# First batch's token softmax built from scores with tokens in partitions, in two halves; seven low-word additions moved from VectorE to GpSimd; the order written anew

## The chip, the cores and the metric

One core of one Trainium2 chip runs the kernel. The metric is the device time of one execution in microseconds; the time of a kernel is the median over several runs. Engines are named as the profile names them: PE (TensorE, its matmuls), PEld (TensorE, its weight loads), DVE (VectorE), ACT (ScalarE), POOL (GpSimd), SP (SyncE, which here issues most loads and stores).

## What is computed

A cross attention between tokens `x` (8 batches, 8 heads, 512 tokens, 64 wide) and states (8 batches, 8 heads, 32 states, 64 wide), and then a feed-forward block over the joined rows:

```
scores  = x @ state^T / 8         a  = softmax over the 32 states      xread = a  @ state
scores2 = state @ x^T / 8         a2 = softmax over the 512 tokens     sread = a2 @ x
rows = concat(xread, sread) by batch, heads joined: 8 x 544 rows of 512
h = rows @ w_in (512 x 2048);  g = h * erf(softplus(h));  out = g @ w_out (2048 x 512)
```

`softplus(h)` is the reference's `max(h,0) + log1p(exp(-|h|))`. Inputs of the attention are float32. The two weight matrices arrive as 64-bit floats and are turned into float32 in the kernel.

## The kernel before

The output rows are worked off batch by batch. The first half of the columns of `w_in` (with the first half of the rows of `w_out`) is pass A, the second half is pass B; stores of B are added to those of A in DRAM. `xread @ w_in` is never formed in two matmuls: for each batch the state is multiplied into `w_in` first (steps `A1m`, `B0m` and so on, buffer `m`), and that is multiplied with the softmaxed scores `y`. Large products go through a Strassen-like scheme of seven products in place of eight (lines 690, 743, 813).

**Batch 0 in pass A is different**, since at the start nothing is loaded: it is done directly, as soon as pieces of weights arrive. This opening, about the first 60 us, is what the change touches. Its steps, by the names that the order uses:

- `lx0`..`lx3` load x of batch 0 (tokens in partitions, two heads each); `lst0` its states; `i0l0`..`i3l1` load the raw 64-bit words of four pieces of `w_in`, `o0l0`..`o3l1` those of `w_out`.
- A piece is converted by `convert` (line 370) in four operations: `a0` (ACT, line 374) from the high words, `a1` (ACT, 376) scales the low words, `v0` (DVE, 378) shifts by three bits, `v1` (DVE, 380) adds the low word. Piece `i0` is done in two halves, `i0` and `i0+`; the others, 128x1024 each, at once.
- `x0`..`x3` (PE, 445) transpose x of two heads each, four 128x128 transposes, into PSUM; `x0c`..`x3c` copy to SBUF (three by DVE, one by ACT). `s0`, `s0c` do it for the states.
- `q0`, `q1` (PE, 460) are the scores of four heads each with states in partitions: 16 matmuls with a 64x32 stationary tile and 128 tokens moving. `q00c` and so on copy them to SBUF.
- `tm0`, `tm1` (PE, 465) transpose these scores, so that tokens stand in partitions. Then comes the softmax over states, once for each group of four heads: `max` (481), `less` (482), `exp` (ACT, 483), `sum` (485), `inv`, `norm` (487); `ta0`, `ta1` (PE, 465) transpose the result back, and `ta0c`, `ta1c` (ACT) copy it to `y`.
- `big0`, `big1`, `big`, `wt`, `wz`, `wn`, `tw` (lines 493 to 506) make the other softmax, over tokens; `rd0` (PE, 525) reads with it.
- `n00`, `n01`, `n02` (piece `i0`, `i0+`, `i1`) and `n10`, `n12` (`i2`, `i3`) multiply the states into `w_in` (PE, 948).
- `h0`..`h7` (PE, 959) are eight products of 128 columns of h for all 512 tokens: two matmuls of 128x128 by 512 each, one for either group of heads. `h0s` is its softplus (ACT, 679), `h0c` its copy (ACT), `h0e` erf for two of them and `h0g` the product with h (DVE, 240).
- `o00`, `o02`, ... (PE, 980) multiply with `w_out`. `a1...` is the attention of batch 1, `A1m` its `m`, `A1f..` its h. `ub` (PE, 1047) turns the states of batch 1. `t..` steps and `T1`..`T4` form sums of `w_out` pieces on DVE.
- `~7*4` is four matmuls of the identity into bank 7: filling that keeps PE running while nothing else is ready. Its line is 427, like that of `warm`.

**What sets the order.** `ORDER` (line 20) is a list of all steps, written out; line 1129 issues them in that order, and `in_order` (line 1120) ties each instruction to the one before it on its engine. So every engine works strictly in the order of the list, and a step that waits holds up all later steps of its engine. Data dependencies across engines become semaphore waits. Loads are issued by SP in the order of the list, too.

Of the kernel before, what the change touches and what calls it, by code (L numbers as in the profile page):

```python
# [10 lines left out]
ALU = mybir.AluOpType  # L11
# [7 lines left out]

ORDER = """  # L20
warm lx0 lst0 lx1 lx2 lx3 i0l0 i0l1 i1l0 i1l1 x0 s0 x1 s0c x0c i2l1 x2 x1c q0 x2c i2l0 x3 q01c
q00c i0a0 big0 tm0 ls1 x3c i0v0 i0a1 max0 q1 i0v1 q11c i3l1 q10c less0 i0+a0 ~7*4 n00 tm1 big1
exp0 i0+v0 i3l0 i0+a1 sum0 big i1a0 inv0 max1 a1xq5 norm0 i1a1 less1 ~6*12 ta0 i1v0 exp1 a1xq4
n00c1 n00c0 sum1 ta0c wt0 inv1 norm1 i2a1 ~7*9 ub i1v1 ta1 i2a0 a1xq1 i0+v1 n02 ta1c i2v0 a1xq0
n02c0 ~6*2 n01 wt1 i2v1 h0 a1xq6 n01c0 i3a0 n01c1 o1l1 wz n02c1 n10 o0l1 i3a1 i3v0 o0l0 h1 n10c1
a1xq7 n10c0 i3v1 h0c o1l0 a1xq3 y01 ~7*2 n12 wn0 h0s h5 y02 h1c n12c1 a1tx2 n12c0 h1s wn1 tw0
a1tx0 tw1 ubc a1xq2 h0e h3 o2l0 tw0c h0g o2l1 tw1c o3l1 o0a0 rd0 a1tx3 y04 o0a1 o0v0 h4 a1x1 rn0
yl0 o1a0 o0v1 rt0 o1a1 h2 o1v0 a1tx1 rc0 o1v1 a1s h5s t01 h7 T1 h5c a2xq2 a1c1 a1c0 o3l0 t02 h3c
t31 a2xq6 h6 hold a1tu0 h3s lst7 h2c a1mx0 lst4 h7c a1tu1 o20 lst1 h4s t32 a2xq1 h7s lst5 a1sb0
h6s a1mx1 a2xq5 lst8 h2s o00 a1my1 lst2 t04 y03 lst3 h2e t34 A1m yk0 a1sb1 lst6 a1x3 h2g t3k a1x2  # L30
a1ex1 a1my0 o02 a1ex0 a1sm1 h4c a1sm0 h6c o10 A1m11 a1iz a1nm1 A1m00 A1m10 a2xq3 a1nm0 a1ey0 o22
a1ta1 a1ey1 a1ta0 a1x0 A1M1 o2a0 A1f01 y11 a1ty1 A1m01 A1f05 a1ty0 A1f0c o2a1 o12 A1M2 a1kz y12
a2xq0 y13 A1M4 t0k A1f06 o2v0 h4e u0 A1M3 y14 A1f02 A1f0u2 a1iy h4g o3a0 A1f07 A1f0c11 o2v1 u1
A1f0u3 A1f11 a1z1 o3a1 A1f0c22 a1z0 A1f04 a1z3 o3v0 h6e a1z2 a2tx0 A1f03 yk1 a2xq4 A1f0c21 o24
o3v1 A1f1c a2xq7 A1f0c12 A1f16 t1k u0c A1f0s22 T2 A1f12 A1f1u2 A1f0s21 A1f17 h6g A1f1c11 A1f0s11
rd1 A1f0s12 u1c t11 A1f1u3 A1f15 T4 a2x3 rn11 rn10 rt1 A1f14 t12 t2k t61 A1e0 o04 a2x2 A1f1c22 t41
a2tx2 A1f13 rc1 A1f1c21 A1g0 a2s o06 A1f1s12 a3xq1 a2c0 A1f1c12 a2c1 a3xq5 t14 A1f1s22 o26 t21
# [12 lines left out]
y33 t54 A3f06 a3ty1 A1bp21 A3M3 A3f0u2 a3kz A3f02 A1bu3 A3M4 a4xq2 A1bc11 A3f07 A1b4 A3f0c11  # L50
A1bc22 A1bp40 A3f0u3 y34 A1b4+ A2e0 A1bp41 A3f0c22 A3f11 A2g1 A3f04 A1bp30 A3f0c21 a3z2 a3iy A3f1c
A3f03 A2g0 a3z0 a3z3 A3f16 A1d3 a3z1 A1bp31 A1d0 A3f1u2 A3f12 A3f0c12 A2q A3f17 A3f1c11 A1bc21
A2ap10 A1bc12 A3f1u3 A2A1 A3f15 A1d1 yk3 A2ap50 a4tx2 A3f0s11 A3f0s12 A3f14 A1D0 A1U2 A2ap11
A3f1c22 A2A3 rd3 A2ac a4tx0 A2ap20 rn31 A1D1 rn30 rt3 A2a2 A2ap21 yl3 rc3 A3f0s21 a4x1 a4s A3f1s11
a4x0 A2A2 A3f1c21 A2ap60 a4c0 A1U3 a4c1 A2ap61 A2a3 A1D2 A3f1s22 A3f1s12 A3f13 a4tu0 A2ap51 A2au2
A1D4 A3f1c12 A2ac11 A2ap70 a5xq2 a4mx0 A3f1s21 A2ap71 A2A4 a5xq7 A1D3 A2bp10 A2au3 A3f0s22 a4sb0
A4m a5xq1 A2a4 a4ex0 A2bp11 A2ac22 A2ap40 A4m00 a5xq6 a4sm0 A4m11 A2ap41 A4m01 A2b2 A4m10 A2ap30
A2ac21 a4iz A2ap31 a4my0 A2bc a5xq5 A2bp20 a4nm0 A2bp60 A3e0 A2ac12 A2bp21 a4ta0 A2bp61 A2bp50
a5xq4 A4M1 A2bc11 A4f01 A2bu2 y41 a4x2 A4M3 A2bp51 a5xq0 A4f0c A4f05 y42 A2b4+ A4M2 A4f02 A2b3
a4ey1 a4x3 A4f06 A2d3 y43 a4ey0 A2bp70 a4ty1 A2d0 A4f0u2 a4ty0 A2bp71 A2b4 A4f07 a4kz A2bu3 y44  # L60
a5xq3 A4f0c11 A2bp40 A4M4 A4f0u3 a4iy A2bc22 A2bp41 A4f0c22 A4f11 A3g0 A3e1 A4f04 A4f03 A2D0
# [12 lines left out]
A5f14 rn51 rn50 A5f1s11 rt5 A5f0s12 A5f1c22 A4ap50 A3D1 rc5 a6tx2 A5f1s22 A4ap11 a6x1 A5f0s22 a6x3
A4a2 A5f13 A4ac a6s A4A2 A4ap60 a6c1 A5f1c12 A5f0s21 A4ap61 A4a3 a6c0 A5f1c21 A4ap20 a7xq0 a6tu0
# [107 lines left out]
def kernel(  # L183
# [8 lines left out]
    nc = tc.nc  # L192
# [971 lines left out]
```

## Time and profile before

| what | value |
|---|---|
| median of 3 runs | 686.01 us (685.63 to 686.43) |
| the profiled execution, its own time | 685.9 us |
| its span, first to last instruction | 684.1 us |
| PE busy over the span | 676.2 us (99%) |
| DVE, ACT, POOL busy | 591.4, 490.9, 87.8 us |
| granted PE clock | 1.00 throughout |
| mean DMA rate | 127 GB/s |

The profile is of one execution. A row of groups gives line, engine, operation, what is written and read, shapes, count, then busy time and mean duration of one, then the engine's idle time ahead of it. The windows view gives the busy time of each engine in a stretch. An instruction's duration contains about 0.09 us in which the next one on the same engine has already started, when nothing makes that one wait; so a queue of DVE instructions moves on by the duration less 0.09. A float32 matmul appears as two records, a transpose as one.

### The profile page before, as it was taken

What the parts mean: (1) busy time and instruction counts of PE and PEld (TensorE: products, weight loads), DVE (VectorE), ACT (ScalarE), POOL (GpSimd) and SP (SyncE); (2) the same over time, 40 slices, a digit from 0 to 9 for tenths busy, and PEclk for the clock granted to TensorE, in tenths of its full rate; (3) what the DMA queues carried; (4) which work ended last, traced back from release to release, by engine and by line L of the source; (5) the groups of instructions that cost most, each with busy time, mean ns of one, the idle gap of its engine ahead of it and who ended that gap; (6) DMA issues with size and microseconds to landing.
All of it is one profiled execution on the core that took longest, in us unless ns stands there. A gap on an engine that the chain in (4) does not pass through costs nothing.

```text
span 684.1 us, 13797 instructions
## 1 busy us (share of the span) xinstructions
PE 676.2 (99%) x5568; PEld 586.8 (86%) x5568; DVE 591.4 (86%) x772; ACT 490.9 (72%) x764; POOL 87.8 (13%) x84
## 2 busy tenths in 40 slices
PE   9999999999999999999999999999999999999997
PEld 7536478989888898999998889898989898989996
DVE  6899999999999999998896699697858795979793
ACT  5999948779787768856785975777674948676821
POOL 0020000030201202021200013010202020201103
PEclk9999999999999999999999999999999999999999
DMA  9896745697777777685975246131514323231427
GB/s 300 203 266 171 153 141 112 182 181 153 182 137 190 118 176 148 185 205 142 214 226 161 78 119 103 34 60 43 60 57 56 72 30 77 29 57 16 78 55 124
DMA packets 145839, 87.15 MB, mean 127 GB/s; under 512 B 92784, under 2 KB 138096, under 8 KB 145776
## 3 DMA queue, kind: packets, MB, share of 16 engines
q1 hardware_dynamic: 126720, 67.78, 36.0%
q0 software_dynamic: 18512, 17.96, 20.4%
q8 instruction: 44, 0.72, 0.4%
q10 hardware_dynamic: 544, 0.52, 0.2%
q14 instruction: 19, 0.16, 0.1%
HBM read 46.14 MB, written 40.11 MB: 126 GB/s over the span
## 4 chain that ended last, share of the span: by engine, by line
PE 88%; ACT 6%; DVE 3%; DMA 1%; issue 1%; SPq 0%; DVEq 0%; ACTq 0%
PE b L813 47%; PE b L690 25%; PE b L743 5%; PE b L1020 4%; PE b L641 4%; DMA big<-in_moe_w_out_dram 1%; ACT ring L679 1%; ACT ring L246 1%; PE b L525 1%; PE b L550 1%; PE b L427 1%; ACT ta L374 0%; ACT L679 0%; ACT ring L974 0%; ACT L575 0%
## 5 line engine op out<-in xcount | busy, mean ns | idle before, releaser
L246 ACT COPY ring<-b 128x512 f32<-128x512 f32 (+1 forms) x144 | 82.4, 584 | 97.5 <-PE b L690 69.5
L813 PE MATMUL b<-big,ring 128*128 128x128 f32 x1196 | 151.9, 275 | 0.0
L721 POOL DMA_DIRECT2D out_dram<-res x67 | 80.3, 1380 | 546.0 <-DVE res L238 150.1
L813 PEld LDWEIGHTS b<-big,ring 128*128 128x128 f32 x1196 | 145.7, 192 | 5.3 <-issue 2.5
L690 PE MATMUL b<-y,m 128*128 128x256 f32 x480 | 121.8, 381 | 0.4 <-DVE y L246 0.3
L690 PEld LDWEIGHTS b<-y,m 128*128 128x128 f32 x480 | 86.2, 190 | 12.4 <-issue 1.6
L246 ACT COPY res<-b 128x512 f32<-128x512 f32 (+2 forms) x125 | 64.2, 524 | 44.7 <-PE b L813 30.7
L690 PE MATMUL b<-sy,m 128*128 128x256 f32 x360 | 91.7, 380 | 0.0
L240 DVE TENSOR_TENSOR ring<-ring 128x2048 f32<-128x2048 f32 (+1 forms) x36 | 78.0, 2167 | 5.2 <-ACT ring L698 3.0
L679 ACT ACTIVATE ring<-ring 128x512 f32<-128x512 f32 x128 | 76.5, 631 | 2.5 <-DVE ring L238 2.1
L813 PE MATMUL b<-ta,ring 128*128 128x128 f32 x548 | 72.8, 276 | 0.0
L690 PEld LDWEIGHTS b<-sy,m 128*128 128x128 f32 x360 | 65.2, 190 | 8.7 <-issue 1.4
L813 PEld LDWEIGHTS b<-ta,ring 128*128 128x128 f32 x548 | 68.0, 192 | 5.4 <-issue 1.7
L238 DVE TENSOR_TENSOR ring<-ring,b 128x512 f32<-128x512 f32 (+1 forms) x72 | 47.2, 660 | 27.7 <-ACT ring L246 10.2
L813 PE MATMUL b<-big,ta 128*128 128x128 f32 x572 | 70.8, 275 | 0.0
L813 PEld LDWEIGHTS b<-big,ta 128*128 128x128 f32 x572 | 68.1, 192 | 2.4 <-ACT b L246 0.8
L239 DVE TENSOR_TENSOR ring<-ring 128x1024 f32<-128x1024 f32 (+3 forms) x66 | 68.6, 1050 | 0.1
L238 DVE TENSOR_TENSOR res<-res,b 128x512 f32<-128x512 f32 (+2 forms) x60 | 36.2, 604 | 29.4 <-ACT res L246 14.2
L698 ACT ACTIVATE ring<-ring 128x2048 f32<-128x2048 f32 x30 | 57.4, 1914 | 0.2
L246 ACT COPY b<-b 128x512 f32<-128x512 f32 (+2 forms) x63 | 34.4, 546 | 14.1 <-PE b L690 8.0
L238 DVE TENSOR_TENSOR res<-res 128x512 f32<-128x512 f32 (+1 forms) x56 | 41.8, 751 | 1.6 <-ACT res L246 1.0
L238 DVE TENSOR_TENSOR ring<-ring 128x1024 f32<-128x1024 f32 (+1 forms) x35 | 39.8, 1141 | 1.0 <-ACT ring L246 0.6
(145 smaller groups left out, 967.7 us busy)
## 6 DMA issues: line engine op xcount, KB each, us to landing
out_dram<-res POOLq DMA_DIRECT2D x63, 256.0 KB, 5.3
out_dram<-res SPq DMA_DIRECT2D x32, 256.0 KB, 3.0
big<-in_x_dram SPq DMA_DIRECT2D x30, 256.0 KB, 4.2
big<-in_x_dram SPq DMA_DIRECT2D x112, 64.0 KB, 3.4
big<-in_moe_w_in_dram SPq DMA_DIRECT2D x12, 512.0 KB, 6.3
big<-in_moe_w_out_dram SPq DMA_DIRECT2D x12, 512.0 KB, 4.9
kept_y<-y SPq DMA_DIRECT2D x8, 512.0 KB, 4.0
y<-kept_y SPq DMA_DIRECT2D x8, 512.0 KB, 4.1
```

Of the source, the lines that this page charges most:

```text
L238: add = lambda o, a, b: tt(o, a, b, op=ALU.add)
L239: sub = lambda o, a, b: tt(o, a, b, op=ALU.subtract)
L240: mul = lambda o, a, b: tt(o, a, b, op=ALU.mult)
L246: do[name] = lambda: f(*args)
L641: pe.matmul(out=to[j][k][Ns * p:Ns * p + Ns, :], lhsT=by, rhs=w_in[r, 4 * j:4 * j + 4, i, :], start=True, stop=True)
L679: act.activation(out=o, in_=i, func=ACTF.Softplus)
L690: pe.matmul(out=to[:, i], lhsT=xs[n - 1][:, q:q + P], rhs=ys[n - 1], start=(start and i == 0), stop=(i == 1), skip_group_check=True)
L698: step(u + "e%d" % o, lambda s=s: act.activation(out=s, in_=s, func=ACTF.Erf))
L721: nc.gpsimd.dma_start(out=to, in_=of, accum_op=ALU.add)
L743: pe.matmul(out=to[:, E2 * h:E2 * h + E2], lhsT=a[:, k // 2, k % 2], rhs=rhs[n][:, k], start=(start and h == 0 and k == 0), stop=(k == 3), ...
L813: pe.matmul(out=out_[:, P * j:P * j + P], lhsT=lhs[:, i], rhs=rhs[:, i], start=(start and j == 0 and i == 0), stop=(i == 1), skip_group_ch ...
L1020: pe.matmul(out=to[:, P * i:P * i + P], lhsT=xs[n - 1][:, i, k], rhs=ys[n - 1][:, k], start=(start and i == 0 and k == 0), stop=(k == 1), ...
```

## The change

**Token softmax.** `tm0` and `tm1` go. New steps `t0`, `t1` compute the scores a second time, with tokens in partitions: `t0` for one half of the tokens (`k` = 0), `t1` for the other, each 16 matmuls with 64x128 of the turned x stationary and 32 states moving, alternating between the upper and the lower 64 rows of PE. The softmax is now done by halves of tokens and not by groups of heads; `max` and `less` are split in two (128x256 each), the rest is as wide as before. `ta0` gives `y` for tokens of the first half, for all heads, so that each `h` product can be split in a left and a right half of the tokens (`h0L`, `h0R`).

**Transposes of x by halves.** `x00`, `x01` and so on: two transposes each and a 128x256 copy each, four by DVE and four by ACT.

**Low words by GpSimd.** In seven pieces (`i1`, `i2`, `i3`, `o0`..`o3`) the step `v1` is issued on POOL.

**Others.** The softmax over tokens works in place; some PSUM banks are named anew; the whole `ORDER` list is another one.

```diff
+BY_GPSIMD = ("i1", "i2", "i3", "o0", "o1", "o2", "o3")
...
-    def convert(name, to, words):
+    def convert(name, to, words, adder=None):
...
-        step(name + "v1", lambda: tt(d, d, lo, op=ALU.add))
+        step(name + "v1", lambda: (adder or dve).tensor_tensor(d, d, lo, op=ALU.add))
...
+        def token_score(k):
+            for h in range(H):
+                at = P * where[h][0] + Ns * where[h][1]
+                for j in range(2):
+                    r = slice(D * j, D * j + D)
+                    pe.matmul(out=token[k, j][:, at:at + Ns], lhsT=xT0[r, h, k],
+                              rhs=st00[r, Ns * h:Ns * h + Ns], start=True, stop=True)
...
+        for k in range(2):
+            step("t%d" % k, token_score, k)
         for g in range(2):
             step("q%d" % g, score, g)
+        for k in range(2):
+            M, Z = (t[:, k].rearrange("p (j f) -> p j f", j=2) for t in (M1, Z1))
+            for j in range(2):
+                of = token[k, j].rearrange("p (f n) -> p f n", n=Ns)
+                step("max%d%d" % (k, j), lambda M=M, of=of, j=j: dve.reduce_max(
+                    out=M[:, j], in_=of, axis=AX.X))
+                step("less%d%d" % (k, j), lambda M=M, of=of, j=j, k=k: sub(
+                    A0[:, k, j].rearrange("p g (q n) -> p (g q) n", n=Ns), of,
+                    M[:, j].unsqueeze(2).to_broadcast([P, H, Ns])))
...
-            step("tm%d" % g, four, bank[6 + g], lambda c, g=g: sc0[:, g, c])
...
-        def first(g, i, to):
+        def first(g, i, to, part):
+            at = slice(256 * part, 256 * part + 256)
             for e in range(2):
-                pe.matmul(out=to, lhsT=X[2 * g + e][:, P * i:P * i + P], rhs=y[0][:, e],
-                          start=(e == 0), stop=(e == 1))
+                pe.matmul(out=to[:, at], lhsT=X[2 * g + e][:, P * i:P * i + P], rhs=y[0][:, e, at],
+                          start=(part == 0 and e == 0), stop=(e == 1), skip_group_check=True)
```

The order of the opening on PE was `x0 s0 x1 x2 q0 x3 tm0 q1 ~7*4 n00 tm1 ~6*12 ta0 ~7*9 ub ta1 n02 ~6*2 n01 h0 n10 h1 ~7*2 n12 h5 tw0 tw1 h3 rd0 h4 rt0 h2 a1s h7 h6 o20 o00 A1m o02`. It becomes `x00 s0 x10 x01 x30 x11 x20 x31 x21 t0 t1 q0 q1 ~7*3 n01 ~7*7 n00 ~7*2 ta0 ~7*7 ta1 h0L n02 ub h0R h1L h1R n10 h2L h3L h3R n12 h2R tw1 tw0 h4L h5L rd0 h7L rt0 h5R a1s h6L h4R h7R h6R o00 ~7*3 o10 A1m`. On DVE, from the first `max` on: `max00 max01 less00 less01 max10 max11 less10 less11 sum0 i0v0 inv0 i0v1 norm0 sum1 q00c inv1 i1v0 norm1 n00c1 q01c big1 big0 big n01c1 i2v0 y01`. On ACT, from the first conversion on: `i0+a0 i0+a1 x21c i0a0 exp0 i0a1 exp1 q10c n01c0 i1a0 i1a1 q11c n00c0 ta0c i2a0 i2a1 ta1c wt1 wt0 i3a0 n02c0 i3a1 h0c`. On POOL: `i1v1 i2v1 i3v1 o0v1 hold lst8 o1v1`, then the other loads `lst`, `o2v1`, `o3v1`.

More of the change, by code (lines that the diff above doesn't have):

```diff
@@ L17 @@
 TWICE = 1
+BY_GPSIMD = ("i1", "i2", "i3", "o0", "o1", "o2", "o3")
 ORDER = """
[L21 to L37, printed above, removed]
@@ L968, in first_unit @@
                 to = bank[k % 6]
-                step("h%d" % k, first, g, i, to)
+                for part in range(2):
+                    step("h%d%s" % (k, "LR"[part]), first, g, i, to, part)
                 step("h%ds" % k, soft, s[:, k], to)
```

357 lines of the change are left out of this document (187 added, 170 removed).

## Prediction

> **What bounds the kernel now.** I read the windows view first. Its columns are: stretch and length in us, then the busy time of PE, PEld, DVE, ACT and POOL with the number of instructions, the granted clock, the DMA share and GB/s.
>
> ```profile
> 0.00:10.00 10.00, 8.55 (x86) 7.07 (x94) 3.72 (x8) 3.03 (x4) 0.69 (x6) 1.00 0.85 268
> 10.00:20.00 10.00, 9.43 (x132) 8.04 (x128) 9.86 (x21) 8.77 (x16) 0.00 (x0) 1.00 1.03 296
> 20.00:30.00 10.00, 10.00 (x94) 4.98 (x79) 8.26 (x18) 9.82 (x16) 0.00 (x0) 1.00 0.77 212
> 40.00:50.00 10.00, 9.42 (x51) 3.58 (x50) 9.20 (x18) 9.94 (x17) 4.51 (x8) 1.00 1.16 268
> 60.00:100.00 40.00, 39.65 (x245) 24.43 (x245) 39.25 (x57) 31.49 (x49) 0.00 (x0) 1.00 0.58 145
> 100.00:200.00 100.00, 100.00 (x990) 87.97 (x989) 98.04 (x124) 77.37 (x129) 12.16 (x10) 1.00 0.74 161
> ```
>
> From 100 us on PE never stops, so the rest of the program lasts as long as its matmuls do. What an edit of the opening is worth is how much earlier PE has its work done when that stretch begins. In the opening a busy PE says little, because filling counts as busy. So I read the timeline of PE next (start, length, line, operation, tiles, shapes).
>
> ```profile
> 13.79 1.50 PE L427 MATMUL b<-ident 128*128 128x128 f32 x12
> 15.28 0.66 PE L465 MATMUL b<-ident,ring 128*128 128x128 f32 x4
> 15.88 2.27 PE L427 MATMUL b<-ident 128*128 128x128 f32 x18
> 18.08 0.45 PE L1047 MATMUL b<-ident,st 128*64 128x64 f32 x8
> 18.49 0.66 PE L465 MATMUL b<-ident,ring 128*128 128x128 f32 x4
> 19.72 0.67 PE L948 MATMUL b<-w_in,st 64*32 64x256 f32 x16 [0.57 <-DVE w_in L380]
> 20.96 0.45 PE L948 MATMUL b<-w_in,st 64*32 64x128 f32 x16
> 21.34 1.98 PE L959 MATMUL b<-y,m 128*128 128x512 f32 x4
> ```
>
> Line 427 is filling, 465 at 15.28 and 18.49 is `ta0` and `ta1`, 959 at 21.34 is `h0`. Pricing every matmul of the first 21.34 us at the spacing it has where PE is full leaves about 13.5 us of filling and idleness. From there to 92 us the same count gives 5 more, and after that nearly none. So at most those 18 us are in play, and chiefly the 13.5 before `h0`. The chain of waits says what makes them: from 8.5 to 19.6 us it runs on DVE almost alone, through the softmax and the `v1` additions. DVE is busy 9.86 of 10 us there. From 30 us on the chain runs on ACT, busy 9.94 of 10.
>
> **Part by part.** The rows that price it (busy us, mean ns of one):
>
> ```profile
> L380 DVE CUSTOM_DVE_ANT_0 w_in<-big,w_in 128x2048 uint16<-128x2048 uint16 x1 | 1.2, 1219 | 0.0
> L246 DVE COPY ring<-b 128x256 f32<-128x256 f32 x2 | 0.8, 420 | 0.3 <-PE b L460 0.3
> masks.py:199 POOL TENSOR_SCALAR_AFFINE_SELECT ident<-ident 128x128 f32<-128x128 f32 x1 | 0.3, 290 | 0.1
> L1047 PEld LDWEIGHTS b<-ident,st 128*64 128x64 f32 x8 | 0.3, 136 | 0.1
> L525 PEld LDWEIGHTS b<-big,ring 128*32 128x32 f32 x64 | 0.9, 110 | 0.8 <-ACT ring L246 0.8
> ```
>
> I lay the new order end to end: a step starts when its engine is free and its inputs are there, with durations from rows (DVE and ACT move on by a duration less 0.09).
>
> *x by halves.* The last two loads of x land at 5.6 and 6.3 us. From 6.35 PE, ACT and DVE pass halves back and forth over four banks (two transposes 0.22, their result 0.3 later, a copy 0.38 on ACT or 0.42 on DVE). The last transpose, `x21`, waits for the copy `x20c` and ends at 7.9. The four ACT copies cost 4 x 0.29 against 0.5 for `x3c`; all but `x21c` lie in ACT's idle time before the first weights (7.8).
>
> *`t0`, `t1`.* No row has a 64-row, 128-column stationary tile with 32 columns moving. A step has 32 records. Upper bound: weight loads of 128 columns follow each other as under line 465 (four in 0.42 us, 0.105 each, 0.11 with its matmul), 3.5 us a step. Lower bound: only the moving matters. Under line 525 a 64-column record takes 0.055 and four tiles run beside each other; 32 columns on two tiles make 0.014 a record, 0.45 a step. I take loads of the upper and lower rows beside each other, two per 0.11 us, so 1.76 a step: lines 1047 and 525 show 8 loads in 0.31 us and 64 in 0.94 us, that is loads of neighbouring tiles overlapping. Then `t0` is 7.9 to 9.7 and `t1` ends at 11.45, with its result at 11.7.
>
> *DVE queue.* `max10` to `less11` are four 128x256 instructions, 4 x 0.33, to 13.05. Then `sum0` .58, `i0v0` .33, `inv0` .45, `i0v1` .6, `norm0` .6, `sum1` .58, `q00c` .33, `inv1` .4, `i1v0` .6, `norm1` .68: 18.15. In the old profile `norm1` ends at 18.44. So dropping `q`, its copies and `tm` from the chain (7.0 to 9.9) buys only 0.3: `t0` and `t1` stand there instead, and DVE keeps its queue.
>
> *PE.* `ta1` 18.4 (its filling ends then), `h0L` 18.85 to 19.7. `ta0c` is long done (ACT 17.0 to 17.6).
>
> *POOL additions.* From the POOL row: by slope over its one-element copy (0.186), 1.03 us for 1024 elements; by whole duration, 8 x 0.29 = 2.3; twice that, 4.6, if two inputs are read in turn. I take 2.3. `i1v0` ends at 17.4, so `i1v1` at 19.75; `n02` 19.85 to 20.45, `ub` to 20.9. `ta1c` ends on ACT at 20.2, after `i2a0` and `i2a1`. So `h0R` is 21.0 to 21.85. The old kernel had the same work done at 21.34 + 1.72 = 23.06. **Lead: 1.2 us.** DVE itself sheds 7 x 1.13 = 7.9 us of queue by 60 us, but few PE steps wait for that queue after `h0`.
>
> The Trainium skill (GPSIMD Engine Reference, 3.1 Elementwise — side-by-side cycle accounting) gives 4497 ns for a two-input addition of 2048 float32 on GpSimd, so an estimate by that page is 2.25 us for one of ours; no run here shows it, and the sum by it is the same.
>
> *Given back later.* `n10` waits for `i2v1` (starts 21.0, ends 23.3) and comes at 23.5, after `h1R`; `n12` at 27 is after `i3v1` (24.3 to 26.6). ACT does not get earlier: it has 1.7 us idle between 10 and 60, and the new order needs the same table loads and conversions. `tw1c` ends there at 31.75 and holds `rd0` about 0.5 us; `o10` waits for `h4s` (42.5), as its bank is that of `h4`, which takes away the rest of the lead: `A1m` starts at about 44.3 against 44.7 now. After `A1m` the old `o02` waits 0.6 us for `h2g` (the waits of PE have it); the new order has `h2g` at 45.4, before `o12` asks. Net lead at 92 us: **0.7 us**. Later orders differ too, but PE is full there: nothing to gain, and a count of changes between steps, each some hundredths of a us, may differ by 0.2. `h` by halves adds 8 starts, below 0.05. The seven `lst` loads stand behind `o1v1` on POOL now; `u0`, which needs them, comes after 50 us, they land before.
>
> Sum: the profiled execution's own time is 685.9 (span 684.1 and 1.8 around it), 0.1 under the median 686.01. 685.9 - 0.7 = **685.2 us**.
>
> **Rivals.**
>
> *Loads of `t` in turn, slower.* Each step 3.5 us in place of 1.76, so `t1` ends at 15.0, all of the DVE queue behind `max10` is 3.5 later, `h0L` at 22.4. The lead becomes a lag of 2.3 to 2.6: 688.5. It decides from about 0.08 us per record. For it: the records of line 465; against it: those of 525. Chance 0.13.
>
> *The additions set the pace, slower.* Between 2.3 and 4.6 us: at 3.0, `n02`, `n10` and `n12` are each 0.7 later in turn, 2.2 in all: 688.1; from 2.5 us on it decides. For it: POOL has no such row, and the only one is short. A form of it: a DVE instruction with two SBUF inputs or a fast one (`norm1`, `y01`, `wn1`) stands still while POOL adds, or POOL behind it. `norm1` would come first and hold `i1v1` 0.6: another 0.4 lost, 685.6. The Trainium skill (SBUF — State Buffer, Who interferes with whom) states that lock: such a DVE instruction and a GpSimd one that reads SBUF exclude each other for whole instructions; nothing in the old trace tests it. Chance 0.20.
>
> *DVE's chain really shortens, faster.* If `t` takes 0.45 to 1 us a step, and additions 1 us, DVE starts `max10` at 10.3 and `h0L` comes at 17.4, held then by filling and DVE. Twice the lead at `h0`, most of it kept: -2.0, 683.9. For it: tiles of line 525 run at the moving rate. Chance 0.19.
>
> **How the numbers follow.** My forecast has 0.48. 0.2% (1.4 us) is about what a measurement of this kernel can tell from no change; 685.2 lies inside. Faster: the last rival and a little of the forecast, 0.22. Slower: the loads in turn and most of the slow additions, 0.29. Same: the rest, 0.49. The range runs from the last rival, 683.9, to the first with the lock, 688.9. That leaves out additions above 3.2 us.
>
> **What would show it.** `h0L` at about 18.9 and `h0R` ending near 21.9; 32 records of line 461 in 1.8 us; POOL additions of 2.3 us; `n02` without a wait of over 0.2; `A1m` at 44.3. Wrong would be: `t1` ending after 13 us, or PE waiting for POOL at `n02`, `n10` and `n12`.

## The result, and the profile after

The changed kernel takes 688.53 us (median of 7 runs, 687.12 to 689.69) against 686.01 us (7 runs, 685.28 to 686.43): a ratio of 1.0036, 95% interval 1.0025 to 1.0048. It is slower by 2.5 us, where 0.8 us less was forecast. The time lies in the forecast's range, and near two of its rivals, but neither rival is what happened.

The profiled execution took 688.63 us (span 686.7). Its windows view, in the columns of before:

```profile
10.00:20.00 10.00, 10.00 (x169) 8.79 (x168) 9.65 (x25) 6.70 (x14) 1.52 (x1) 0.83 1.12 336
20.00:30.00 10.00, 10.00 (x96) 7.14 (x96) 8.00 (x13) 9.70 (x16) 5.75 (x3) 1.00 0.85 184
40.00:50.00 10.00, 10.00 (x62) 5.33 (x61) 9.82 (x18) 9.95 (x15) 6.53 (x9) 1.00 0.98 200
100.00:200.00 100.00, 99.22 (x977) 86.83 (x976) 96.83 (x122) 75.48 (x123) 12.17 (x10) 1.00 0.75 162
```

Two numbers are new in the first row. The granted clock is 0.83, where before had 1.00, and ACT is busy 6.70 us of 10, where it had 8.77. PE looks busier (10.00 for 9.43), but filling counts as busy. Between 100 and 200 us the one thing new is a wait of PE of 0.8 us. The timeline of PE shows where the opening goes:

```profile
8.20 3.76 PE L461 MATMUL b<-st,big 64*128 64x32 f32 x64
11.89 2.13 PE L469 MATMUL b<-big,st 64*32 64x128 f32 x64
13.95 1.65 PE L433 MATMUL b<-ident 128*128 128x128 f32 x6
15.53 0.45 PE L969 MATMUL b<-w_in,st 64*32 64x128 f32 x16
15.91 1.83 PE L433 MATMUL b<-ident 128*128 128x128 f32 x14
18.60 0.60 PE L474 MATMUL b<-ident,ring 128*128 128x128 f32 x4
20.60 0.60 PE L474 MATMUL b<-ident,ring 128*128 128x128 f32 x4
21.03 1.03 PE L981 MATMUL b<-y,m 128*128 128x256 f32 x4
...
22.97 2.86 PE L981 MATMUL b<-y,m 128*128 128x256 f32 x12
...
29.14 0.66 PE L969 MATMUL b<-w_in,st 64*32 64x256 f32 x16
...
33.63 1.10 PE L546 MATMUL b<-big,ring 128*32 128x64 f32 x64 [0.17 <-ACT ring L251]
```

Line 461 is `t0` and `t1`, 469 `q0` and `q1`, 433 filling (two records for each product), 969 `n01` (at 29.14 `n12`), 474 `ta0` and `ta1`, 981 `h0L` (from 22.97 on `h0R`, `h1L`, `h1R`), 546 `rd0`. `ta0` starts at 18.60, although DVE had `norm0` ready at 15.91; `ta1` starts at 20.60, although `norm1` ended at 18.66. What stands ahead of both is filling. The three products of filling behind the scores take 1.65 us; without the clock's fall they take 0.94 (below).

**PE has no gap from 8.2 us to 33.46 us, filling included.** So here a delay ahead of `h0R` reaches `n12` and `rd0` in full. Followed back from `rd0`, the chain of waits runs on ACT to 29.84 us (the copy of `n12`, a table load of 1.28 us, four short operations), and from there on PE alone back to 8.27 us, with 5.5 us of filling in it.

The clock, microsecond by microsecond in the same execution (the figure behind POOL):

```profile
12.00:13.00 1.00, 1.00 (x42) 0.96 (x48) 1.00 (x4) 0.83 (x2) 0.00 (x0) 0.56 1.11 352
14.00:15.00 1.00, 1.00 (x7) 1.00 (x6) 0.97 (x5) 0.42 (x2) 0.00 (x0) 0.50 1.08 317
15.00:16.00 1.00, 1.00 (x20) 0.58 (x19) 1.00 (x3) 0.00 (x0) 0.00 (x0) 0.74 1.10 340
```

The shares give 0.88 + 2 + 0.52 = 3.4 us at half clock, right behind 3.7 us of `t0` and `t1`. And in the last row ACT does nothing at all. So the next view is what ACT waited for from 8 to 31 us, and its busy time in two stretches:

```profile
ACT m L251 <- PE b L969: 1.9, 2, 1.6
ACT w_in L379 <- DMA big<-in_moe_w_in_dram: 1.3, 1, 1.3
ACT ring L498 <- DVE ring L244: 1.1, 1, 1.1
ACT y L251 <- PE b L474: 0.4, 1, 0.4
```

```profile
8.00:30.00 22.00, 22.00 (x293) 17.76 (x293) 18.52 (x40) 17.56 (x30) 7.27 (x3) 0.92 0.99 269
30.00:45.00 15.00, 14.83 (x136) 10.69 (x136) 12.77 (x22) 14.91 (x23) 7.39 (x8) 1.00 0.94 262
```

The same stretch of the kernel before:

```profile
8.00:30.00 22.00, 21.06 (x242) 14.05 (x225) 19.77 (x42) 20.15 (x33) 0.00 (x0) 1.00 0.92 262
```

**ACT stands idle 22 - 17.56 = 4.44 us between 8 and 30 us, where it stood idle 1.85 us before: 2.59 us more.** The two profiled executions differ by 688.63 - 685.9 = 2.73 us. From 30 us on ACT is busy 14.91 of 15 us, so what it lost is not made up. It waits for products that it has to copy, `n01` (1.6 us in one piece) and `ta0`, which stand on PE behind the filling; for `exp0`'s input from DVE (1.1 us); and for the first weights, with which it starts at 8.84 us and not at 7.82: 0.84 of the 4.44 us. All steps of an engine go in the order of the list, so the large conversions `i1a0`, `i1a1`, which need nothing from PE, stand behind the small copy `n01c0`.

### The profile page after: what moved, and what is told of

It is laid out like the page before. It is cut to its first block, busy times and chain, and to the rows that moved or that the text cites. A ratio compares the mean times of both kernels' runs of the same rounds, so it can differ in the third digit from the quotient of the medians.

```text
span 686.7 us, 13956 instructions
## 1 busy us (share of the span) xinstructions
PE 679.2 (99%) x5642; PEld 594.6 (87%) x5642; DVE 589.8 (86%) x770; ACT 498.6 (73%) x773; POOL 104.6 (15%) x91
## 4 chain that ended last, share of the span: by engine, by line
PE 90%; ACT 3%; issue 3%; DMA 1%; POOL 1%; DVE 1%; SPq 0%; DVEq 0%; POOLq 0%; ACTq 0%
PE b L834 47%; PE b L711 24%; PE b L764 5%; PE b L1043 4%; PE b L662 4%; PE b L981 2%; PE b L546 1%; PE b L571 1%; PE b L433 1%; DMA big<-kept_z 1%; DMA big<-in_x_dram 1%; ACT ring L700 1%; POOL ta L385 1%; ACT ring L719 1%; PE b L461 1%
## 5 line engine op out<-in xcount | busy, mean ns | idle before, releaser
L251 ACT COPY b<-b 128x512 f32<-128x512 f32 (+2 forms) x63 | 34.3, 546 | 14.4 <-PE b L711 7.5
```

The source lines that it names most:

```text
L251: do[name] = lambda: f(*args)
```

## The experiments

The first theories were two. *Theory 1:* the sparse products of `t0` and `t1` let the granted clock fall, and the fixed filling behind them then holds `ta0` and `ta1`. *Theory 2:* the additions on GpSimd set the pace, with the lock that they put on DVE. A third came with the runs: what counts is how long ACT is left without work. All ratios below are to the kernel before on the same chip; intervals are 95%.

### Additions: a_dve_adds, b_old_order_gpsimd

`a_dve_adds` is the changed kernel with

```diff
-BY_GPSIMD = ("i1", "i2", "i3", "o0", "o1", "o2", "o3")
+BY_GPSIMD = ()
```

> The changed kernel with all low-word additions back on VectorE, in the same order. Theory 1 (the granted clock falls to 0.5 for one window after the sparse token-score products, and the filling in strict order then holds the two transposes of the weights): the filling is untouched, so ta0 and ta1 stay near 18.6 and 20.6 us and the time stays at 688.0 to 689.0 us. Theory 2 (the 2.4-us GpSimd additions, and the VectorE operations that they lock, 2.27 us for y01 and 1.81 us for wz, set the pace): without them the time falls to 687.3 us or less.

Measured: 688.18 us, 1.0031 (1.0020 to 1.0043). The interval overlaps that of the changed kernel: theory 2 does not hold in this order. The clock stayed at 1.00 in the profiled run, so it also shows the filling and `ta1` at full speed:

```profile
13.48 0.94 PE L433 MATMUL b<-ident 128*128 128x128 f32 x6
...
19.41 0.60 PE L474 MATMUL b<-ident,ring 128*128 128x128 f32 x4
```

`b_old_order_gpsimd` is the kernel before, order and all, with only this changed, for the same seven names:

```diff
-        step(name + "v1", lambda: tt(d, d, lo, op=ALU.add))
+        step(name + "v1", lambda: (adder or dve).tensor_tensor(d, d, lo, op=ALU.add))
```

> The kernel before, in its own order, with only the additions of i1, i2, i3 and o0 to o3 moved to GpSimd. Theory 2 (the additions and their lock): slower than the kernel before by 1.3 us or more, 687.3 us or above, since each addition takes 2.4 us in place of about 1.1 us and i1v1, i2v1, i3v1 stand ahead of products of the opening. Theory 1 (clock and filling): the additions are beside the path, 685.5 to 686.5 us.

Measured: 688.89 us, 1.0044 (1.0031 to 1.0058), as theory 2 has it. So the additions cost 2.9 us in the old order and nothing that can be told in the new one. The lock itself is in both traces. In the changed kernel, DVE and then POOL:

```profile
22.43 2.27 DVE L244 TENSOR_TENSOR sy<-y 128x256 f32<-128x256 f32 x1 [0.67 <-ACT y L251]
...
26.89 1.81 DVE L428 TENSOR_SCALAR z<-z 128x2 f32<-128x2 f32 x1
```

```profile
22.01 2.41 POOL L385 TENSOR_TENSOR w_in<-w_in,ring 128x1024 uint32<-128x1024 uint32 x1 [1.07 <-ACT ring L381]
26.27 2.41 POOL L385 TENSOR_TENSOR w_in<-w_in,ring 128x1024 uint32<-128x1024 uint32 x1 [1.85 <-ACT ring L381]
```

A subtraction that takes 0.42 us in `a_dve_adds` takes 2.27, an operation on 128x2 that takes 0.16 before takes 1.81; the one ends 0.28 us behind the addition, the other with it. In the changed kernel neither is in the chain of waits. In `b_old_order_gpsimd` the same happens inside the softmax, 1.76 us for `inv1`, which takes 0.17 before:

```profile
17.10 1.76 DVE L426 TENSOR_SCALAR z<-z 128x16 f32<-128x16 f32 x1
```

### Filling: c_no_filling, d_filled_scores

`c_no_filling` drops `~7*3`, `~7*7`, `~7*2`, `~7*7` of the opening from the order:

```diff
-exp1 ~7*3 n01 ... norm0 ~7*7 n00 ... sum1 ~7*2 ta0 ... q01c ~7*7 ta1
+exp1 n01 ... norm0 n00 ... sum1 ta0 ... q01c ta1
```

> The changed kernel without the 19 filling products of its opening (~7*3, ~7*7, ~7*2, ~7*7). Theory 1: n01 follows q1 at 14 us, ta0 follows norm0 at 16 us, ta1 follows norm1 at 18.7 us, h0L starts by 19.3 us in place of 21.03, and the time falls by 1.2 to 1.8 us, to about 687.0 us; if the clock falls in more windows for want of filling, by up to 3.4 us at half speed, the time is 688 us or above and the granted clock below 0.995. Theory 2: the additions hold n02 and what follows, so at most 0.5 us is gained, 688.0 to 688.5 us.

Measured: 689.68 us, 1.0050 (1.0038 to 1.0063). The second branch of theory 1 came: in the profile the clock is at 0.5 from about 11 us for 13.6 us, four times the 3.4 us. So the filling helps to keep the clock; but one of the five runs (688.37 us) held 1.00 without it, so it is not all that decides.

`d_filled_scores` puts a full-height product between the scores:

```diff
                     pe.matmul(out=token[k, j][:, at:at + Ns], lhsT=xT0[r, h, k], ...)
+                if h % 2:
+                    warm(bank[3][:, 0:P], 1)
```

> The changed kernel with one 128-column product on a free bank after every second head of the token scores: 8 more products of about 0.112 us, 0.9 us in all. Theory 1: the granted clock stays at 1.0 from 5.3 us on, q0 and q1 take 1.25 us in place of 2.06, the 19 filling products take 0.112 us each in place of up to 0.214, and ta1 comes about 1 us earlier in spite of the 0.9 us added; 687.0 to 688.0 us. Theory 2: only the 0.9 us is added, 688.5 to 689.5 us.

Measured: 695.02 us, 1.0137 (1.0123 to 1.0151), far outside both expectations. PE's timeline in it:

```profile
8.39 0.64 PE L461 MATMUL b<-st,big 64*128 64x32 f32 x8
8.96 0.49 PE L433 MATMUL b<-ident 128*128 128x128 f32 x2
9.37 0.63 PE L461 MATMUL b<-st,big 64*128 64x32 f32 x8
```

A group starts every 0.98 us. Its eight records take 8 x 0.0575 = 0.46 and the filling 0.22, so 0.30 us is left for the two changes between 64-row and 128-row tiles. The clock falls here too, at about 12.8 us.

### The clock: g_scores_in_turn, k_half_height, l_sparse_in_before

`g_scores_in_turn` moves `q0` between `t0` and `t1`, and `q1` right behind `t1`:

```diff
-... i0+a0 t0 ls1 ... i0a0 t1 max00 ... less01 q0 max10 exp0 q1 max11 ...
+... i0+a0 t0 q0 ls1 ... i0a0 t1 q1 max00 ... less01 max10 exp0 max11 ...
```

> The changed kernel with q0 between t0 and t1 and q1 right behind t1, so that no stretch of 3.4 us holds sparse token-score products alone. Theory 1 (a window that is nearly all token scores lets the clock fall): the granted clock stays at 1.0 in the opening in most runs (0.998 and above over the run), t1 ends 0.7 us later and the softmax's second half with it, the filling runs at full speed, and the time is 687.0 to 688.2 us. Rival (the clock falls for another reason): clock of 0.996 as in the changed kernel, and 688.5 to 689.5 us.

Measured: 688.94 us, 1.0049 (1.0037 to 1.0062). Mean clocks of its six runs: 1.000 twice, 0.997, and 0.993 to 0.995 three times. It separates nothing; the profiled run, with the clock held, took 687.92.

`k_half_height` adds filling of the scores' own shape:

```diff
+                for j in range(2 * (h % 2)):
+                    r = slice(D * j, D * j + D)
+                    pe.matmul(out=bank[3 + j][:, 0:P], lhsT=xT0[r, h, k], rhs=ident[r],
+                              start=True, stop=True)
```

> The changed kernel with filling of the same shape as the token scores: after every second head the same two 64-row stationary tiles move 128 more columns into free banks, 16 more products in all, in row-group pairs of about 0.115 us each, so 0.9 us in all and without a change of the stationary tile's height. Theory 1 (columns moving per time keep the clock): the granted clock stays at 1.0 behind the scores in most runs, 0.998 or above, q0 and q1 take 1.4 us, and the time is 687.0 to 688.3 us in spite of the 0.9 us. Rival (filling does not keep the clock there): 0.996 or less, 689.0 to 689.8 us.

Measured: 688.22 us, 1.0033 (1.0021 to 1.0045). The mean clock was 0.998 or above in all five runs, where the changed kernel had 0.995 or 0.996 in six of seven, and 1.00 throughout the profiled opening. That part of theory 1 held, as far as a mean over the run can say: the profiled run of `m_no_late_filling` has 0.998 and one fall of 3.4 us. The price of the filling was 0.225 us a pair, 1.8 us in all and not 0.9. So `h0L` starts at 22.04, 1.0 us later than in the changed kernel, and `A1m` at 47.45, again 1.0 later: PE is as full there, and what the clock no longer took, the new filling did. The total is the same because the profiled changed kernel lost 1.0 us behind `A1m` (below). ACT's waits in it from 8 to 31 us have changed places:

```profile
ACT ring L502 <- DVE ring L244: 3.7, 2, 2.2
ACT m L251 <- PE b L973: 0.9, 2, 0.6
```

ACT waits 2.6 us longer for its scores and 1.0 us less for `n01` and its like.

`l_sparse_in_before` was to put products of the scores' shape into the kernel before, in place of its filling ahead of `ta0` (`~s*3` issues 48 of them, on the turned x):

```diff
-... less1 ~6*12 ta0 ...
+... less1 ~s*3 ta0 ...
```

> The kernel before with its 12 filling products ahead of ta0 (2.84 us) replaced by 48 products in the shape of the token scores (64x128 stationary, 32 columns moving, 0.0575 us each, 2.8 us). Theory 1 (the shape of the work lowers the clock): the granted clock falls to 0.5 for one window of 3.4 us behind them in most runs, clock 0.995 to 0.997 over the run, and the time rises by 0.5 to 1.5 us to 686.5 to 687.5 us. Rival (the shape is harmless): clock 0.998 to 1.0 and 685.5 to 686.2 us.

Measured: 701.42 us, 1.0217 (1.0204 to 1.0231). This run is spoilt: loads for batch 1 (`a1xq5` stands ahead in the order) write where the turned x was, so the products waited 7.3 us for a transfer, and the time says nothing. Its clock says something that was not planned. PE was idle from 14.4 us to 21.7 and the clock fell; then the sparse products ran until 30.4 us:

```profile
24.00:28.00 4.00, 4.00 (x42) 4.00 (x40) 0.00 (x0) 0.00 (x0) 0.00 (x0) 0.50 0.02 4
28.00:32.00 4.00, 4.00 (x30) 3.94 (x29) 0.00 (x0) 0.49 (x2) 0.00 (x0) 0.50 0.33 53
32.00:36.00 4.00, 4.00 (x44) 3.31 (x43) 1.07 (x2) 3.27 (x6) 0.00 (x0) 0.79 0.77 149
```

PE is 4.00 busy of 4.00, and stays at half clock for the 8.7 us of sparse products and until 33.7 us, 3.3 us after denser work began. So in this execution 8.7 us of products with 32 columns moving, one close behind the other, did not bring the clock back.

### The later order: e_kept_first, f_old_order_later

PE's waits in the changed kernel's profile have one row that before has not, at about 135 us:

```profile
PE b L546 <- DMA big<-kept_z: 0.8, 1, 0.8
```

Six loads of `a4xq1`, `a4xq2`, `a4xq0` stand ahead of the reloads of `kept_z` on SP's queue. `e_kept_first` moves them behind:

```diff
-a3kz ... A3M3 a4xq1 A3f06 ... A3f0c11 a4xq2 ... A3f07 a4xq0 ... a3z1
+a3kz ... A3M3 A3f06 ... A3f0c11 ... A3f07 ... a3z1 a4xq1 a4xq2 a4xq0
```

> The changed kernel with the three steps a4xq1, a4xq2 and a4xq0 (six transfers on SyncE's queue) moved behind the four reloads of kept_z of batch 3, as the kernel before had all but one of them. Theory (part of the loss is in the new order behind the opening): the reloads are issued at about 130.5 us in place of 133.6, TensorE's wait of 0.8 us at L546 goes, and the time falls by 0.6 to 0.8 us, to about 687.8 us. Rival (the wait only takes the place of a wait that comes anyway): within 0.2 us of the changed kernel.

Measured: 687.55 us (12 runs), 1.0036 (1.0021 to 1.0051). The reloads go out at 130.9 us and the wait is gone, but the ratio, with one run of 693.36 us in it, is that of the changed kernel. By medians it lies 1.75 us above the kernel before on its chip and the changed kernel 2.52, so the times do not decide between theory and rival. But the profiles of `a_dve_adds`, `c_no_filling`, `d_filled_scores`, `g_scores_in_turn`, `h_less_filling` and `k_half_height`, which keep the changed order there, do not have this wait at all. So it is no fixed part of the loss; of the kept profiles only that of the changed kernel has it.

`f_old_order_later` keeps the changed order up to `rd0` and then goes on in the relative order of before.

```diff
-... o0v1 rd0 h1s o3l1 h7L rn0 a1tx3 ... (order of after)
+... o0v1 rd0 h5R h1s a1tx0 h0e h0g o3l1 ... (order of before)
```

> The changed kernel's order up to and with rd0 (33 us), and all steps behind it in the relative order of the kernel before, so without the changed kernel's last filling (~7*3) too. Theory (opening alone): if the whole loss is in the first 33 us, the time stays at 688.0 to 689.0 us. Rival (the new order later costs what the count of TensorE's spare time suggests, 0.7 us between 32 and 60 us and 0.9 us between 104 and 144 us): 686.9 to 687.4 us. If the old order suits the new opening badly, above 689 us.

Measured: 690.96 us, 1.0079 (1.0062 to 1.0097), with a wait of 2.4 us for the transposed reads of batch 0, and in the profiled run a second fall of the clock between 35 and 45 us. The old order does not suit the new opening; it tells nothing on where the loss is.

### Less filling and additions: h_less_filling, i_less_and_kept, j_h0_early, m_no_late_filling, p_dve_w_in

`h_less_filling` is `g_scores_in_turn` with

```diff
-exp1 ~7*3 n01 ... norm0 ~7*7 n00 ... sum1 ~7*2 ta0 ... q01c ~7*7 ta1
+exp1 n01 ... norm0 ~7*4 n00 ... sum1 ta0 ... q01c ~7*5 ta1
```

> As the kernel before it in this list (q0 between t0 and t1), with 9 filling products in place of 19 in the opening (none ahead of n01 and ta0, 4 ahead of n00, 5 ahead of ta1). Theory 1: ta1 follows norm1 at about 19.3 us, h0L 1.0 to 1.5 us earlier than with all the filling, 686.5 to 687.2 us, if the clock holds; if too little filling lets the clock fall behind the scores, more than 688.5 us with a granted clock under 0.996. Rival (the filling does not hold the path): within 0.3 us of the kernel with all the filling.

Measured: 688.13 us, 1.0037 (1.0024 to 1.0051); 687.2 to 688.5 but for the profiled run, 690.43, which waited 1.4 us for x and lost the clock for three stretches. Nothing is settled by it.

`i_less_and_kept` is `e_kept_first` with

```diff
-norm0 ~7*7 n00 ... sum1 ~7*2 ta0 ... q01c ~7*7 ta1
+norm0 ~7*4 n00 ... sum1 ta0 ... q01c ~7*2 ta1
```

> The changed kernel with the reloads of kept_z of batch 3 ahead of a4xq1, a4xq2, a4xq0, and with 9 of the opening's 19 filling products (3 ahead of n01, 4 ahead of n00, none ahead of ta0, 2 ahead of ta1). Theory (fixed filling holds ta0 and ta1, and the reloads cost 0.8 us later): h0L 1.2 to 2 us earlier than in the changed kernel, and 0.8 us saved at 135 us, 686.0 to 686.8 us. Rival (only the reloads count): 687.5 to 687.9 us. If less filling lets the clock fall for more than one window: 688 us or above with a granted clock of 0.994 or less.

Measured: 687.03 us, 1.0019 (1.0010 to 1.0027). Its eleven runs are two groups: seven from 686.70 to 687.05 with a mean clock of 0.997 to 0.999, and four from 688.18 to 688.89 at 0.993 to 0.995. The profiled one, 688.49, has half clock from 11.8 to 18.7 us, twice 3.4 us. What the two groups differ by, some 1.5 us, is then the price of one or two such falls: at 0.998 one fall can still be in a run.

`j_h0_early` goes further and puts `h0L` ahead of `ta1` and its filling, `ta0c` and the copy `n00c0` ahead of `i1a1`, `i2a0` behind `ta1c`, and (not in the lines shown) `ub`, `h0R`, `h1L` and `h1R` ahead of `n02`:

```diff
-norm0 ~7*4 n00 i1a1 sum1 ta0 ... n00c0 i1v0 ta0c a1xq3 norm1 i2a0 n00c1 i1v1 q01c ~7*2 ta1 big1 i2a1 h0L
+norm0 ~7*4 n00 sum1 ta0 ... n00c0 ta0c i1a1 q11c inv1 n00c1 i1v0 a1xq3 norm1 n01c1 i1v1 q01c h0L ~7*2 ta1
```

> As the kernel before it, but with real work in place of the filling ahead of ta1: the copies n00c0, ta0c and n00c1 are moved ahead of i1's conversion and of norm1, h0L (0.9 us) goes ahead of ta1, and h0R, h1L and h1R go ahead of n02. Theory: h0L starts at 18.4 to 19.2 us and TensorE has 3.6 us of products until the 2.4-us addition of i1 ends, 685.3 to 686.5 us. Rival (i1's and i2's pieces, now later by about 1 us on ScalarE and GpSimd, hold n02 and n10): 687 us or above, with a wait of TensorE for w_in.

Measured: 688.23 us, 1.0029 (1.0019 to 1.0038): the rival. `h0L` started at 17.75 us, 3.3 us earlier than in the changed kernel, and `rd0` at 33.33, 0.3 us earlier. PE waited for ACT (1.4 us) and for additions on GpSimd (1.1 us) in between.

`m_no_late_filling` is `i_less_and_kept` without `~7*3` ahead of `o10`:

```diff
-lst7 ~7*3 o10
+lst7 o10
```

> The changed kernel with the reloads of kept_z first, 9 of the opening's 19 filling products, and without the last filling (~7*3, 0.67 us of TensorE at 44.0 us, ahead of o10). Theory (that filling is pure cost, since o10 could run): 0.5 to 0.7 us less than the kernel with it, 686.0 to 686.3 us in runs whose clock holds. Rival (o10 waits for h4s until then anyway, so the filling covers a wait): no change, 686.7 to 687.0 us in runs whose clock holds.

Measured: 687.32 us (12 runs), 1.0017 (1.0009 to 1.0026); the five runs at 0.998 and 0.999 lie within 686.43 to 686.56, some 0.4 us under those of `i_less_and_kept`. From `rd0` to `A1m` it takes 12.43 us in place of 12.82: the filling is 0.67 us of PE, of which 0.4 was cost.

`p_dve_w_in` is `m_no_late_filling` with three additions back on DVE:

```diff
-BY_GPSIMD = ("i1", "i2", "i3", "o0", "o1", "o2", "o3")
+BY_GPSIMD = ("o0", "o1", "o2", "o3")
```

> As the first kernel of this list, with the additions of i1, i2 and i3 on VectorE, those of o0 to o3 still on GpSimd. Theory 2 in what it may still hold (once the filling does not, the 2.4-us additions hold n02 and n10 and lock y01 and wz): TensorE's waits for w_in go and the time falls by 0.4 to 1 us, to 685.5 to 686.2 us in runs whose clock holds. Rival (VectorE's own work, 1.1 us more for each piece, comes late by as much): within 0.3 us.

Measured: 686.48 us, 1.0010 (1.0001 to 1.0018), the best of the changed orders and surely better than the changed kernel. Nine of its eleven runs lie within 686.14 to 686.85; against the five runs of `m_no_late_filling` just named that is no difference, so the rival has it for the additions. Its median is lower because the clock went to 0.995 or below in two runs of eleven, and in six of twelve there; whether the additions have to do with that is not shown.

### What was still open: n_half_height_few, q_all_three, r_read_later, s_first_half_early

`n_half_height_few` is `m_no_late_filling`, and `q_all_three` is `p_dve_w_in`, with the filling of `k_half_height` after every fourth head only:

```diff
+                for j in range(2 * (h % 4 == 3)):
```

> As the kernel before it, with half-height filling after every fourth head of the token scores: four pairs of products that move 128 more columns, 0.225 us each, 0.9 us in all. Theory 1 (columns moving keep the clock): the granted clock is 0.998 or above in most runs, the runs lie within 0.5 us of each other, and the median is 0.2 to 0.9 us above the held-clock runs of the kernel without it, 686.3 to 687.2 us. Rival (four pairs are too few): the clock still falls in about half the runs, 687.5 to 689 us in those.

> Both together: the additions of i1, i2 and i3 on VectorE and the four pairs of half-height filling. If the three causes (clock, filling and reloads, additions) add up: 685.5 to 686.5 us with a clock of 0.998 or above, about level with the kernel before or faster. If something else in the new order costs: 686.8 us or above even with the clock held.

Measured: 687.73 us, 1.0026 (1.0016 to 1.0036), and 687.43 us, 1.0024 (1.0013 to 1.0035). In four of 12 and in five of 12 runs the clock still fell to 0.994 or 0.995, 2 us dearer each time. Four pairs are too few, and cost more than they save.

`r_read_later` is `p_dve_w_in` with

```diff
-h2s a1tx2 o0v1 rd0 h1s o3l1 h7L rn0 a1tx3 h0e rt0 h5R
+h2s a1tx2 o0v1 h5R rd0 h1s o3l1 h7L rn0 a1tx3 h0e rt0
```

> The kernel with the reloads first, less filling and the additions of w_in on VectorE (p_dve_w_in), with h5R moved from behind rt0 to ahead of rd0. Theory (part of the lead is given back at rd0, where TensorE waits 0.5 us for tw1c of ScalarE): the wait goes, 0.3 to 0.5 us less, 685.9 to 686.2 us in runs whose clock holds. Rival (rd0 later only makes the chain rn0, rt0, rc0 and the scores of batch 1 later): no change or up to 0.5 us more.

Measured: 686.67 us, 1.0015 (1.0006 to 1.0024). PE's wait of 0.5 us for `tw1c` is gone, and no time with it: rival.

`s_first_half_early` is `r_read_later` (so `h5R` stands ahead of `rd0`) with `h0L` ahead of `ta1`, and `ub` and `h0R` ahead of `n02`:

```diff
-norm0 ~7*4 n00 i1a1 sum1 ta0 ... n00c0 i1v0 ta0c a1xq3 norm1 i2a0 n00c1 i1v1 q01c ~7*2 ta1 big1 i2a1 h0L
+norm0 ~7*4 n00 sum1 ta0 ... n00c0 ta0c i1a1 q11c inv1 n00c1 i1v0 a1xq3 norm1 i1v1 q01c h0L ta1 ta1c i2a0
```

> The kernel p_dve_w_in with n00c0, ta0c and n00c1 ahead of i1's conversion and of norm1, h0L ahead of ta1 in place of the last two filling products, and h0R ahead of n02. Theory (TensorE's 1.3 us of waiting for norm1 at ta1 can be filled, and what is gained there is kept): 0.4 to 0.9 us less, 685.5 to 686.0 us in runs whose clock holds. Rival (ScalarE's queue, full from 16 to 30 us, sets rd0, so that all of the lead is given back there): within 0.2 us of p_dve_w_in, 686.2 to 686.6 us, with a longer wait at rd0.

Measured: 688.41 us, 1.0034 (1.0022 to 1.0045). The profiled run, 688.41, lost the clock and waited 1.0 us for x as well; its `rd0` is at 35.15 us (`r_read_later`: 33.11), and its `h0L`, at 19.85, no earlier than there (19.28). The fastest of its runs, 686.64, is no faster than those of `r_read_later` and `p_dve_w_in`: the expected gain did not come.

### What the runs have in common

None of the runs was made for ACT. But in all their profiles the stretch from 8 to 30 us can be read as above. In `d_filled_scores`, the worst, it is

```profile
8.00:30.00 22.00, 21.98 (x248) 17.91 (x250) 12.91 (x32) 10.53 (x18) 3.19 (x2) 0.77 0.78 225
```

| profiled run | its time | ACT idle, 8 to 30 us | time less idle | `h0R` starts | `rd0` starts |
|---|---|---|---|---|---|
| before | 685.9 | 1.85 | 684.05 | | 31.35 |
| a_dve_adds | 687.20 | 3.40 | 683.80 | 21.78 | 32.54 |
| j_h0_early | 687.48 | 4.02 | 683.46 | 20.81 | 33.33 |
| g_scores_in_turn | 687.92 | 4.33 | 683.59 | 22.80 | 33.46 |
| after | 688.63 | 4.44 | 684.19 | 22.97 | 33.63 |
| e_kept_first | 688.08 | 4.56 | 683.52 | 23.53 | 34.19 |
| i_less_and_kept | 688.49 | 4.92 | 683.57 | 23.64 | 34.30 |
| k_half_height | 688.69 | 5.22 | 683.47 | 23.98 | 34.64 |
| h_less_filling | 690.43 | 6.24 | 684.19 | 25.32 | 35.98 |
| d_filled_scores | 695.00 | 11.47 | 683.53 | 30.22 | 40.88 |
| without `~7*3`: p, r, n, m, q | 686.27, 686.67, 686.82, 686.50, 686.98 | 3.77, 3.76, 4.05, 4.11, 4.45 | 682.39 to 682.91 | 21.32 to 22.49 | 32.84 to 33.49 |
| without `~7*3`: s | 688.41 | 4.95 | 683.46 | 22.47 | 35.15 |

Over idle times from 3.4 to 11.5 us the fourth column moves by 0.7 us: what ACT idles in the opening, the whole is longer by. With DVE's idle time in its place, the eight of these that have all the additions on GpSimd give 683.5 to 685.9, so ACT's fits better. The fit does not make it the cause. ACT has nearly the same work ahead of `rd0` in all these kernels, so whatever delays what it works on shows as its idle time; no run here gives ACT other work to do. Nor does all of it fit. The five without `~7*3` lie 1 us lower, of which that filling explains 0.4. Four more do not fit: `c_no_filling` (685.40) with waits of PE of 0.6 and 0.5 us more, `f_old_order_later` (686.12) with its wait of 2.4, `b_old_order_gpsimd` (685.86) with PE's wait of 1.5 for the locked softmax, and the spoilt `l_sparse_in_before` (686.34).

**PE's columns say where the delay comes from.** From `h0R` to `rd0` it takes 10.66 to 10.76 us in eight of the kernels, whatever the time, and 12.8 from `rd0` to `A1m` in all of these: what makes `h0R` late makes the whole late. In the changed kernel, `e_kept_first` and `k_half_height` that is PE itself, full with scores and filling; their chain of waits lies on PE up to `n12`. In `a_dve_adds` and `p_dve_w_in`, whose clock stayed at 1.00, the chain runs on DVE, to the end of `big` at 21.6 and 21.8 us, then on ACT to `rd0` at 32.54 and 32.84. So filling at the fallen clock holds `rd0` at 33.63, and 0.8 to 1.1 us ahead of that the queues of DVE and ACT hold it. That is why less filling, and `h0L` earlier, gained less than it freed on PE. That DVE's and ACT's queues set those 32.5 us is read from the chains; no run makes them lighter. No version here beats the kernel before.

## Why the prediction was wrong

- *What bounds it, and PE full from 100 us on.* Right. From `A1m` to the end it takes 641.2 us before, 641.2 in `k_half_height`, and 642.2 in the profiled changed kernel, with its 0.8 of `kept_z`.
- *x by halves, `t0`, `t1`.* Right. The 64 records took 3.69 us (forecast 3.52) and `t1` ended at 12.0 (11.45). With it both rivals on `t` fall: loads were not in turn (0.115 us for two), and the moving did not set the pace.
- *DVE's queue.* Right within 0.5 us: `less11` ended at 13.46 (13.05), `norm1` at 18.66 (18.15). The chain was late because `i0+a0` started at 8.84 and not 7.8: its weights landed at 8.81 us, before at 7.80. With the old order of loads ACT's first conversion starts at 8.55 in `b_old_order_gpsimd` and at 8.45 in `l_sparse_in_before`, so most of that may be chance between executions.
- *"`ta1` 18.4 (its filling ends then)", and from it "Lead: 1.2 us".* **This is the step that failed first.** `ta1` came at 20.60. Two parts. At full clock (`a_dve_adds`) it is 19.41: the scores end 0.7 us later than forecast there, and behind them come 7.3 us of products and filling that nothing shortens. And the clock was taken as granted at 1.00, since all of the trace before shows 1.00 there; the opening with the new shape let it fall, and that added 1.2 us. `h0R` began at 22.97 and not at 21.0, and was done at about 23.9 where the kernel before had the same work done at 23.06: a lag of 0.8 us and no lead. With no gap on PE up to `rd0`, this went through: `n12` at 29.14 (27), `tw1c` done at 33.57 (31.75).
- *POOL additions.* Right, 2.40 us for 2.3. `i1v1` ended at 20.94 (19.75) because its input `i1a1` came from ACT at 18.40. **The rival of additions that set the pace** forecast 688.1 and the time came near it, and the lock that it names is in the trace; but `a_dve_adds` shows that it costs nothing here that can be told. (Where the filling no longer holds `h0L`, `n02` does wait 0.4 to 0.8 us for the addition, in `g`, `h`, `i`, `j`, `m` and `n`.) Nor does the rival's own sum give 688.1: 2.2 us on 685.2 are 687.4. A time that fits is no proof of its cause. The Trainium skill (SBUF — State Buffer, Who interferes with whom) has this lock as whole-instruction exclusion; the trace agrees, 2.27 us for 0.42.
- *Given back later.* **This step failed in a smaller part.** It gave ACT the idle time of the old order ("it has 1.7 us idle between 10 and 60") and so put `tw1c` at 31.75, `rd0` right behind and `A1m` at 44.3. ACT's idle time between 10 and 60 us was 4.09 us in the new order, and `A1m` came at 46.45, 2.15 us later than forecast. Of the 1.82 us at `tw1c`, 1.08 go when the clock holds: in `a_dve_adds` it is done at 32.49. The other 0.74 stand there with the chain of waits on DVE and ACT; the forecast had not laid out DVE's queue behind `norm1`. Another 0.4 is `~7*3`, which was not priced. From `A1m` to the end it took 642.2 us and not 640.9: 0.8 is the wait for `kept_z`, the other 0.5 was not traced. The lead that the forecast counted on, `h0L` earlier, was bought in `j_h0_early` and is worth nothing.
- *Later orders: nothing to gain.* Right but for that one wait: 641.2 us from `A1m` on in both orders.

Open: why the clock falls in some runs and not in others of the same kernel (in the profiles that lose it behind the scores, it goes between 11.0 and 12.9 us, and never for less than 3.4 us; in `a_dve_adds`, `j_h0_early`, `p_dve_w_in` and `r_read_later` the same scores left it at 1.00); why `rd0` comes no earlier than 32.5 us when it holds, as what remains of ACT's idle time in `p_dve_w_in`, 3.77 us, was not taken apart; and the lateness of the first weights.

## What to carry to other kernels

Filling is not free in a strict order: it is a wait of fixed length, here 7.3 us with the products between, and it takes longer when the clock falls. So lay out the engine that carries it like any other, and ask what the forecast becomes if the clock is not granted. Then find the engine that is saturated behind the stretch that you edit, and lay out its queue in the new order too; its idle time in the old order says nothing of the new. A short copy that waits for another engine holds up all the long work behind it, so long work that needs nothing from others is a candidate for a place in front of it; that was not tried here.

## What the hardware showed that was not expected

- A PE that the profile shows as busy can lose the granted clock. It fell behind 3.7 us of closely packed products with few columns moving, with no gap on PE, in some executions and not in others, and 8.7 us of them did not bring it back. It stayed down for 3.4 us (five profiles, behind the scores), 6.8 (`i_less_and_kept`), 10.2 (`d_filled_scores`, `h_less_filling`), 13.7 (`c_no_filling`) and 17.1 (`l_sparse_in_before`, where PE had stood idle first): once to five times 3.4. The Trainium skill (TensorE: Matmul & The Clock Gate, Part 1) has the gate fall after an idle window of about 3.4 us and rise after a busy one; the length agrees, 3.4 us, but "busy" in the profile is not all that the gate goes by.
- Going from 64-row to 128-row tiles and back cost 0.30 us for the pair of changes (`d_filled_scores`, what is left of 0.98 us for a group when its products are taken off). The Trainium skill (TensorEngine Tiling (Array Packing), Key Properties) says that a change of tiling mode drains TensorE; the trace agrees, as far as a remainder can show it, and gives the price.
- The lock between DVE and POOL caught even an operation on two numbers per partition: 1.81 us for 0.16.
